# HGRN2 outer-product attention followed by a SERF feed-forward: from the ninth chunk on, the cumulative sums of log f from two 12-bit parts in float32r, logits kept for three chunks

## The chip, the cores and the metric

One core of one Trainium2 chip runs the kernel. The metric is device time in microseconds (us) of one execution, as the median of several runs.

## The reference

Inputs are q, k, v and f_logit, each of shape (4 batches, 8 heads, 768 steps, 48), and the weights w_in (384 x 2048) and w_out (2048 x 384). Per batch and head a 48x48 state is carried over the 768 steps:

```python
f = 1 / (1 + exp(-f_logit))
state = f[t][:, None] * state + outer(k[t], v[t])
y[t] = q[t] @ state
```

The 8 heads of 48 are put side by side to 3072 tokens of 384 numbers (x), and these go through

```python
h = x @ w_in
g = h * erf(softplus(h))
out = g @ w_out
```

## The kernel before, in words

**Units.** The steps of a batch are taken in chunks of 128 tokens, numbered 0 to 23 over the four batches (`g`). Two chunks are a block of 256 tokens (`CPB = 2`, `TB = 256`), so there are 12 blocks.

**A chunk's attention** goes through five steps:

- `prepare` makes log(1/f) of the logits in place: `clamp` (VectorE, L363), then `logs`, an Exp (ScalarE, L371) and a Ln (L372), on both chunks of a block at a time (128x768) except at the start. `logs` first loads another activation table (L351).
- `stage_d` (L386) takes the cumulative sums over the tokens of each half chunk as one product with a triangle of ones, `tri` (L391, 128x128 by 128x384, float32, into `ps_d`). ScalarE makes exp(-sum) (`dp`, L394) and exp(sum) (`kd`, L397) of it, eight small DMAs on the queue of SyncE (SP) carry each chunk's total decays to `Tall` (L402), and VectorE multiplies with q and k (`qd` L406, `kd` L410).
- `stage_t` transposes `qd` and `kd` on TensorE (L422) and copies the results out (L429, L433). It also runs the second half of the state update of the chunk before (`late`).
- `stage_s` makes the state's increments (L469) and the scores (L477), masks the scores (VectorE L505, by a triangle `tri1`), and updates the state (`next_state`: VectorE L446 and L447, then two GpSimd copies L449 into `sv`).
- `stage_y` makes y from scores, v and state (L534) into `xT`. The left operand `sv` holds v, which DMAs put there, beside the state.

**The feed-forward.** `hidden` makes h = x @ w_in for a block in four groups (L596). The activation of a group is a generator stepped by `act_step`: Exp (L157), two Tanh (L160), two products (VectorE L165), a Tanh (L568), a last product (VectorE L570). `project_first` (L686, blocks 0 and 1) and `project` (L737, the others, with seven products of half blocks in place of eight, from sums made by VectorE at L624) multiply by w_out; the results are put together at L745 and L753 and stored (L663).

**Order.** Each engine runs its own instructions in program order, which is written out by hand. In iteration `it` (0 to 11) a generator yields once for each product or two of the feed-forward; the slot number `s` counts these, and the steps of the attention, the loads and the steps of the activation are placed at given slots. Iteration `it` runs the attention of block `it + 2`, the hidden products of block `it + 1`, the projection of block `it - 2` and the logarithms of block `it + 3`. From iteration 4 on the slots of the attention's steps are

```python
at = [2, 26, 42, 54, 76, 90]   # d of the odd chunk, t, y and s, d of the next block's even chunk, t, y and s
```

`prepare_at` is the slot of that second `stage_d` less 14: `clamp` runs at `prepare_at - 6`, `logs` at `prepare_at`.

**Loads.** q, k, v, f_logit and w_in, w_out come by DMAs from the SP queue, in program order, except two at the start. The logits of a block lie in a tile `lt` of two chunks, of which there are two (`lpool`, four chunks in all). They are loaded (`load_f`, L229) in the middle of the iteration before the one that takes their logarithms. The weights are loaded in 16 pieces (L296) and put together from 64-bit words by ScalarE and VectorE (L315 to L340) during the first 130 us.

Of the kernel before, what the change touches and what calls it, by code (L numbers as in the profile page):

```python
# [42 lines left out]

FP32 = mybir.dt.float32
I32 = mybir.dt.int32
U32 = mybir.dt.uint32
U8 = mybir.dt.uint8
# [27 lines left out]
def kernel(  # L75
# [32 lines left out]

    def fixed(name, shape, dtype=FP32, pool=const):
        return pool.tile(shape, dtype, name=name)  # L110
# [58 lines left out]

    main = ExitStack()  # L170
    fix = main.enter_context(tc.tile_pool(name="fix", bufs=1))
    lpool = main.enter_context(tc.tile_pool(name="lpool", bufs=2))
# [46 lines left out]
    FIRST = 3  # L219


    lts = {}

    def load_f(g):
        b, c = divmod(g, NCH)
        blk, j = divmod(g, CPB)
        if j == 0:
            lts[blk] = lpool.tile([P, CPB, d_model], FP32, name="lt", tag="lt")
        nc.sync.dma_start(  # L229
            out=lts[blk][:, j, :].rearrange("t (h d) -> t h d", d=D), in_=heads(f_logit, b, c)  # L230
        )

    def load(g, what="qkv", queue=None):
        b, c = divmod(g, NCH)
# [9 lines left out]
    def half(c):  # L244
        return slice(C * c, C * (c + 1))

    def load_sv(g):
        b, n = divmod(g, NCH)
        for r in range(2):
            for c in range(2):  # L250
                to = svs[g % NSV][half(1 - r), r, c, :, PAD : PAD + D]
# [107 lines left out]
        sets[0] = 0  # L359

    def clamp(blk, j0, j1):
        lt = lts[blk][:, j0:j1, :].rearrange("t j c -> t (j c)")
        nc.vector.tensor_scalar(  # L363
            out=lt, in0=lt, scalar1=LOGIT_MIN, scalar2=None, op0=ALU.max
        )

    def logs(blk, j0, j1):

        lt = lts[blk][:, j0:j1, :].rearrange("t j c -> t (j c)")
        use_exp_ln()  # L370
        nc.scalar.activation(out=lt, in_=lt, func=AF.Exp, scale=-1.0)  # L371
        nc.scalar.activation(out=lt, in_=lt, func=AF.Ln, bias=1.0)  # L372
# [12 lines left out]
    def stage_d(g):  # L385
        blk, j = divmod(g, CPB)  # L386
        if g < FIRST:
            ps = ps_moe.tile([P, 2, 512], FP32, name="ps_d0", tag="moe")[:, 0, 0:d_model]
        else:
            ps = ps_at.tile([P, 512], FP32, name="ps_d", tag="at")[:, 0:d_model]  # L390
        nc.tensor.matmul(ps, lhsT=tri[:], rhs=lts[blk][:, j, :], start=True, stop=True)  # L391
        dp = dps[g % 2]
        kd = kds[g % 2][:, :, 0:D]
        nc.scalar.activation(  # L394
            out=dp[:, :, 0:D], in_=ps.rearrange("t (h d) -> t h d", d=D), func=AF.Exp, scale=-1.0
        )
        nc.scalar.activation(out=kd, in_=ps.rearrange("t (h d) -> t h d", d=D), func=AF.Exp)  # L397
        if g >= FIRST:
            for c in range(2):
                end = C * (c + 1)  # L400
                for a in range(HP):
                    nc.sync.dma_start(  # L402
                        out=Tall[:, g, c, a : a + 1],
                        in_=dp[end - 1 : end, 2 * a : 2 * a + 2, :].rearrange("o r d -> o (r d)"),
                    )
        nc.vector.tensor_tensor(  # L406
            out=qd[:, :, 0:D], in0=qns[g % NQ][:].rearrange("t (h d) -> t h d", d=D),
            in1=dp[:, :, 0:D], op=ALU.mult,
        )
# [27 lines left out]
    def next_state(k, dS):  # L437

        g, c = divmod(k, 2)
        g1, c1 = divmod(k + 1, 2)  # L440
        total = Tall[0:STATE, g, c, :].unsqueeze(2).broadcast_to((STATE, HP, D))
        add = dS[0:STATE, c, :].rearrange("p (a d) -> p a d", a=HP)
        if k % (2 * NCH) == 0:
            nc.vector.tensor_tensor(out=state[0:STATE], in0=add, in1=total, op=ALU.mult)
        else:
            nc.vector.tensor_tensor(out=state[0:STATE], in0=add, in1=state[0:STATE], op=ALU.add)  # L446
            nc.vector.tensor_tensor(out=state[0:STATE], in0=state[0:STATE], in1=total, op=ALU.mult)  # L447
        for r in range(2):
            nc.gpsimd.tensor_copy(  # L449
                out=svs[g1 % NSV][rows(r), r, c1, :, PAD : PAD + D], in_=state[rows(r)]  # L450
            )

    def stage_s(g):
        b, n = divmod(g, NCH)
        last = n == NCH - 1
        if n == 0:
            for r in range(2):
                nc.gpsimd.memset(svs[g % NSV][rows(r), r, 0, :, PAD : PAD + D], 0.0)
# [34 lines left out]
        for c in range(2):  # L493
            for r in range(2):
                if FIRST <= g < 2 * ADJACENT:

                    nc.scalar.copy(out=qA[half(1 - r), r, :, half(c)], in_=sc[half(c), r])
                    if c == 1:
                        flat = qA[half(1 - r), r].rearrange("s a (c t) -> s (a c) t", c=2)
                        nc.gpsimd.affine_select(  # L500
                            out=flat, in_=flat, pattern=[[0, 2 * HP], [1, C]], compare_op=ALU.is_ge,
                            fill=0.0, base=0, channel_multiplier=-1,
                        )
                    continue
                nc.vector.tensor_tensor(  # L505
                    out=qA[half(1 - r), r, :, half(c)], in0=sc[half(c), r],
                    in1=tri1[half(c)].unsqueeze(1).broadcast_to((C, HP, C)), op=ALU.mult,
                )
        next_state(2 * g, dS)
        if not last:  # L510
# [2 lines left out]
    def stage_y(g):  # L513
# [17 lines left out]
        for n in range(len(todo[0])):  # L531
            for i in todo:
                c, kt, a, r, o = todo[i][n]
                nc.tensor.matmul(  # L534
                    y[M * i : M * (i + 1), kt, half(c)], lhsT=sv[:, r, c, a, o : o + M],
                    rhs=qA[:, r, a, half(c)], start=(n == 0), stop=True, skip_group_check=True,
                )
        nc.scalar.copy(out=xTs[blk][:, :, j * P : (j + 1) * P], in_=y[:])  # L538
# [280 lines left out]
    with tc.manual_schedule():  # L819

        for t in svs:
            nc.vector.memset(t[:].rearrange("p r c a d -> p (r c a d)"), 0.0)
        use_exp_ln()
        load_f(0)
        load(0, "kv", nc.scalar)
# [6 lines left out]
        load(2)  # L832
        load_piece(1)
        load_piece(2)
        load_f(3)
# [52 lines left out]
        keep_busy(10)  # L888
        prepare(0, 0, 1)
        stage_d(0)  # L890
        keep_busy(6)
        prepare(0, 1, 2)
        stage_t(0)
# [1 line left out]
        load_piece(3)  # L895
        stage_d(1)
        prepare(1, 0, 1)
        load_f(4)
        load_f(5)
        load_sv(0)  # L900
        stage_s(0)
        weights_steps(2)
# [1 line left out]
        load(4, "qk")  # L904
        load_piece(4)
        stage_d(2)
        load_sv(1)
        weights_steps(2)
        stage_y(0)
# [30 lines left out]
        for it in range(n_blocks):  # L940
# [16 lines left out]
            for s, _ in enumerate(gen):  # L957
# [6 lines left out]
                if at and s == at[0]:  # L964
                    at.popleft()
                    f, g = todo.popleft()
                    f(g)
                    if f in (stage_y, stage_y_s):
                        if g + NSV < n_chunks:
                            load_sv(g + NSV)  # L970
                        load_to(g + LOOK)
                        if g == 2:
                            load(5, "v")
                            load_piece(7)
                if it == 0 and s == 14:
                    prepare(2, 0, CPB)
                if it == 0 and s == 9:
                    load_f(6)
                    load_f(7)
                if s == n // 2 and it + 4 < n_blocks:  # L980
                    for j in range(CPB):
                        load_f((it + 4) * CPB + j)
                if it + 3 < n_blocks and s == prepare_at - 6:
                    clamp(it + 3, 0, CPB)
                if it + 3 < n_blocks and s == prepare_at:
                    logs(it + 3, 0, CPB)
                if it < 2:
                    step = it == 1 and s % 6 == 3
                elif it == 2:
# [240 lines left out]
```

## Time and profile before

| | |
|---|---|
| median of 3 runs | 612.42 us (612.28 to 612.85) |
| the profiled execution | 612.61 us, of which its span is 610.9 us |
| TensorE (PE) busy | 588.6 us, 96% of the span |
| VectorE (DVE) busy | 428.7 us, 70% |
| ScalarE (ACT) busy | 382.7 us, 63% |
| GpSimd (POOL) busy | 92.8 us, 15% |
| mean granted clock of TensorE | 0.984 of full speed |
| HBM read and written | 35.59 and 4.72 MB |

The profile is of one execution. Times are in us from its start unless marked ns. PE are TensorE's matrix products, PEld its loads of the left operand, which run beside them; SPq is the DMA queue of SyncE. A float32 product on PE stands in the profile as two MATMUL instructions, each with its weight load. "idle before <-" names the releaser of the idle time just before an instruction. In lines of groups, xN is the number of instructions, followed by busy time and mean duration.

### The profile page before, as it was taken

What the parts mean: (1) busy time and instruction counts of PE and PEld (TensorE: products, weight loads), DVE (VectorE), ACT (ScalarE), POOL (GpSimd) and SP (SyncE); (2) the same over time, 40 slices, a digit from 0 to 9 for tenths busy, and PEclk for the clock granted to TensorE, in tenths of its full rate; (3) what the DMA queues carried; (4) which work ended last, traced back from release to release, by engine and by line L of the source; (5) the groups of instructions that cost most, each with busy time, mean ns of one, the idle gap of its engine ahead of it and who ended that gap; (6) DMA issues with size and microseconds to landing.
All of it is one profiled execution on the core that took longest, in us unless ns stands there. A gap on an engine that the chain in (4) does not pass through costs nothing.

```text
span 610.9 us, 13911 instructions
## 1 busy us (share of the span) xinstructions
PE 588.6 (96%) x5729; PEld 514.6 (84%) x5729; DVE 428.7 (70%) x702; ACT 382.7 (63%) x483; POOL 92.8 (15%) x121
## 2 busy tenths in 40 slices
PE   8797999998999999999999999999999899999996
PEld 7575888887656789989989989989989889989996
DVE  4888996674697588777777586767685675657551
ACT  5834566978875688856766767856856466266000
POOL 1333032234123101302002200102001200000000
PEclk9978999999999999999999999999999999999999
DMA  9998854431221322412412413313211000000000
GB/s 209 259 235 232 225 137 80 80 54 32 49 53 28 79 38 42 80 36 45 80 33 47 77 30 53 71 35 55 53 28 14 2 27 0 27 1 1 27 27 30
DMA packets 155605, 41.37 MB, mean 68 GB/s; under 512 B 147344, under 2 KB 150416, under 8 KB 155536
## 3 DMA queue, kind: packets, MB, share of 16 engines
q1 hardware_dynamic: 153312, 39.82, 29.8%
q8 instruction: 47, 0.77, 0.5%
q10 hardware_dynamic: 2224, 0.59, 0.4%
q14 instruction: 22, 0.18, 0.1%
HBM read 35.59 MB, written 4.72 MB: 66 GB/s over the span
## 4 chain that ended last, share of the span: by engine, by line
PE 81%; DVE 7%; ACT 7%; issue 2%; POOL 2%; ACTq 0%; POOLq 0%; DVEq 0%
PE hps L596 37%; PE ops L737 25%; PE ops L686 5%; PE y L534 3%; PE ps_t L422 3%; PE ps_d L391 2%; PE sc L477 2%; PE sc L469 2%; POOL sv L449 2%; ACT x L160 1%; DVE qA L505 1%; DVE Hg L570 1%; ACT e L568 1%; PE busy L383 1%; ACT e L157 1%
## 5 line engine op out<-in xcount | busy, mean ns | idle before, releaser
L596 PE MATMUL hps<-xT,w_in_sb 128*128 128x256 f32 x1152 | 266.1, 387 | 2.4 <-ACT xT L538 1.2
L596 PEld LDWEIGHTS hps<-xT,w_in_sb 128*128 128x128 f32 x1152 | 219.2, 193 | 36.6 <-ACT xT L538 1.9
L165 DVE SCALAR_TENSOR_TENSOR e<-x,e 128x1024 f32<-128x1024 f32 x96 | 117.2, 1221 | 13.9 <-ACT x L160 13.8
L449 POOL COPY sv<-state 48x192 f32<-48x192 f32 x88 | 76.3, 867 | 319.0 <-DVE state L447 222.9
L160 ACT ACTIVATE x<-Hg,serf_bias 128x1024 f32<-128x1024 f32 x88 | 97.5, 1141 | 0.2
L157 ACT ACTIVATE e<-Hg 128x1024 f32<-128x1024 f32 x44 | 46.5, 1058 | 52.3 <-DVE Hg L570 48.3
L737 PE MATMUL ops<-wT,Hg 128*128 128x192 f32 x320 | 78.4, 328 | 0.0
L570 DVE TENSOR_TENSOR Hg<-Hg,e 128x1024 f32<-128x1024 f32 x44 | 53.7, 1221 | 24.6 <-ACT e L568 24.5
L737 PE MATMUL ops<-wT,scratch 128*128 128x192 f32 x288 | 67.8, 326 | 0.9 <-DVE scratch L745 0.9
L603 ACT COPY Hg<-hps 128x1024 f32<-128x1024 f32 x44 | 44.4, 1010 | 36.2 <-PE hps L596 35.8
L737 PE MATMUL ops<-w_out_sb,Hg 128*128 128x192 f32 x320 | 65.1, 326 | 0.0
L737 PEld LDWEIGHTS ops<-wT,Hg 128*128 128x128 f32 x320 | 55.7, 190 | 1.9
L737 PEld LDWEIGHTS ops<-w_out_sb,Hg 128*128 128x128 f32 x320 | 54.6, 190 | 2.0
L505 DVE TENSOR_TENSOR qA<-sc,tri 64x256 f32<-64x256 f32 x68 | 28.7, 422 | 34.1 <-PE sc L477 33.1
L568 ACT ACTIVATE e<-e 128x1024 f32<-128x1024 f32 x48 | 50.3, 1048 | 1.9 <-DVE e L165 1.8
L737 PEld LDWEIGHTS ops<-wT,scratch 128*128 128x128 f32 x288 | 50.2, 190 | 1.1 <-issue 1.1
L745 DVE TENSOR_TENSOR scratch<-scratch,ops 128x384 f32<-128x384 f32 (+1 forms) x40 | 19.9, 497 | 33.4 <-ACT scratch L753 26.0
L406 DVE TENSOR_TENSOR qd<-qn,dp 128x384 f32<-128x384 f32 x24 | 13.9, 580 | 39.0 <-ACT dp L394 39.0
L534 PEld LDWEIGHTS y<-qA,sv 128*32 128x32 f32 x1536 | 24.3, 111 | 19.6 <-issue 8.9
L534 PE MATMUL y<-qA,sv 128*32 128x64 f32 x1536 | 29.0, 222 | 10.8 <-POOL sv L449 5.1
L429 ACT COPY qA<-ps_t 64x512 f32<-64x512 f32 x48 | 27.7, 577 | 16.9 <-PE ps_t L422 16.6
L737 PE MATMUL ops<-w_out_sb,scratch 128*128 128x192 f32 x132 | 32.2, 326 | 0.0
(118 smaller groups left out, 653.2 us busy)
## 6 DMA issues: line engine op xcount, KB each, us to landing
lt<-in_f_logit_dram SPq DMA_DIRECT2D x24, 192.0 KB, 3.8
qn<-in_q_dram SPq DMA_DIRECT2D x24, 192.0 KB, 3.2
kn<-in_k_dram SPq DMA_DIRECT2D x23, 192.0 KB, 3.5
vt<-in_v_dram SPq DMA_DIRECT2D x23, 192.0 KB, 3.7
out_dram<-scratch SPq DMA_DIRECT2D x11, 384.0 KB, 2.6
sv<-in_v_dram SPq DMA_DIRECT2D x84, 48.0 KB, 2.9
w_out_sb<-in_moe_w_in_dram SPq DMA_DIRECT2D x4, 768.0 KB, 6.0
Hg<-in_moe_w_in_dram SPq DMA_DIRECT2D x4, 768.0 KB, 6.3
```

The lines of the kernel that those rows point to most:

```text
L157: nc.scalar.activation(out=dst[:], in_=h, func=AF.Exp)
L160: nc.scalar.activation(out=dst[:], in_=h, func=AF.Tanh, bias=serf_bias[:, i : i + 1], scale=SERF_KAB[i][0])
L165: nc.vector.scalar_tensor_tensor(out=e[:], in0=x[:], scalar=SERF_KAB[i][2], in1=e[:], op0=ALU.add, op1=ALU.mult)
L449: nc.gpsimd.tensor_copy(out=svs[g1 % NSV][rows(r), r, c1, :, PAD : PAD + D], in_=state[rows(r)])
L505: nc.vector.tensor_tensor(out=qA[half(1 - r), r, :, half(c)], in0=sc[half(c), r], in1=tri1[half(c)].unsqueeze(1).broadcast_to((C, HP, C)), ...
L534: nc.tensor.matmul(y[M * i : M * (i + 1), kt, half(c)], lhsT=sv[:, r, c, a, o : o + M], rhs=qA[:, r, a, half(c)], start=(n == 0), stop=Tru ...
L568: nc.scalar.activation(out=e[:], in_=e[:], func=AF.Tanh, scale=SERF_C)
L570: nc.vector.tensor_tensor(out=h, in0=h, in1=e[:], op=ALU.mult)
L596: nc.tensor.matmul(hps[:, j, :], lhsT=w_in_sb[:, kt, ft * P : (ft + 1) * P], rhs=xTs[blk][:, kt, :], start=(kt == 0), stop=(kt == n_k - 1),)
L603: nc.scalar.copy(out=gr["h"], in_=hps[:])
L686: nc.tensor.matmul(ops[:, tt, 0:d_model], lhsT=gr["h"][:, j, tt * P : (tt + 1) * P], rhs=w_out_sb[:, ft, :], start=(ft == 0), stop=(ft == ...
L737: nc.tensor.matmul(place[n], lhsT=x[:, j, :], rhs=y, start=(gi == 0 and j == 0 and n in first), stop=(gi == n_g - 1 and j == 1), skip_grou ...
```

## The change

From block 4 (`SPLIT`), that is from chunk 8 of 0 to 23, log(1/f) is split before the triangular product: a VectorE copy rounds it to float32r (the upper part), a VectorE subtraction leaves the remainder (the lower part, also float32r), and `stage_d` sums the two products of `tri_r`, the triangle in float32r, in one PSUM tile. Blocks 0 to 3 keep the one float32 product. The first part's copy and subtraction stand in program order right behind `logs` of the block; those of the second chunk stand 18 slots later, because there is one buffer `parts` for both.

The logits lie in a ring of three chunks, in place of two tiles of two. Their loads move: chunk 3 behind `stage_d(0)`, chunks 4 and 5 behind `stage_d(2)`, chunk 7 from slot 9 of iteration 0 to slot 36, chunks 8 and 9 from slot 48 to slot 78, and both chunks of blocks 5 to 11 from the middle of the iteration before to just behind the first `stage_d` of the iteration that uses them, behind that step's eight small DMAs.

The tiles `sv` are packed closer (272 in place of 320 numbers for a part), and the mask of the scores is read from `tri` in place of a copy `tri1`.

```diff
-    tri1 = fixed("tri1", [P, C])
+    tri_r = fixed("tri_r", [P, P], FP32R)
...
-    svs = [fixed(f"sv{i}", [P, 2, 2, HP, D + 2 * PAD], pool=fix) for i in range(NSV)]
+    svs = [fixed(f"sv{i}", [P, 2, 2, HP * DP + PAD], pool=fix) for i in range(NSV)]
...
+    SPLIT = 4
+    NL = 3
+    lring = fixed("lt", [P, NL, d_model], pool=fix)
+    parts = fixed("parts", [P, 2, d_model], FP32R, pool=fix)
+
+    def lt_of(blk, j0, j1):
+        if blk == SPLIT:
+            return lring[:, 2 * j0 : 2 * j1 - 1 : 2, :]
+        s = (CPB * blk + j0) % NL if blk < SPLIT else j0
+        assert s + j1 - j0 <= NL
+        return lring[:, s : s + j1 - j0, :]
...
+    def split(g):
+
+        blk, j = divmod(g, CPB)
+        x = lt_of(blk, j, j + 1)[:, 0]
+        nc.vector.tensor_copy(out=parts[:, 0], in_=x)
+        nc.vector.tensor_tensor(out=parts[:, 1], in0=x, in1=parts[:, 0].bitcast(FP32), op=ALU.subtract)
...
-        nc.tensor.matmul(ps, lhsT=tri[:], rhs=lts[blk][:, j, :], start=True, stop=True)
+        if blk < SPLIT:
+            nc.tensor.matmul(ps, lhsT=tri[:], rhs=lt_of(blk, j, j + 1)[:, 0], start=True, stop=True)
+        else:
+            for i in range(2):
+                nc.tensor.matmul(ps, lhsT=tri_r[:], rhs=parts[:, i], start=(i == 0), stop=(i == 1))
...
-                    in1=tri1[half(c)].unsqueeze(1).broadcast_to((C, HP, C)), op=ALU.mult,
+                    in1=tri[half(c), half(c)].unsqueeze(1).broadcast_to((C, HP, C)), op=ALU.mult,
...
-        for c in range(2):
-            nc.gpsimd.tensor_copy(out=tri1[half(c), :], in_=tri[half(c), half(c)])
+        nc.gpsimd.tensor_copy(out=tri_r[:], in_=tri[:])
...
                     f, g = todo.popleft()
                     f(g)
+                    if f is stage_d and g % CPB and SPLIT < it + 3 < n_blocks:
+                        for j in range(CPB):
+                            load_f((it + 3) * CPB + j)
...
                 if it == 0 and s == 9:
                     load_f(6)
+                if it == 0 and s == 36:
                     load_f(7)
-                if s == n // 2 and it + 4 < n_blocks:
-                    for j in range(CPB):
-                        load_f((it + 4) * CPB + j)
+                if it == 0 and s == 78:
+                    load_f(8)
+                    load_f(9)
                 if it + 3 < n_blocks and s == prepare_at - 6:
                     clamp(it + 3, 0, CPB)
                 if it + 3 < n_blocks and s == prepare_at:
                     logs(it + 3, 0, CPB)
+                    if it + 3 >= SPLIT:
+                        split((it + 3) * CPB)
+                if SPLIT <= it + 3 < n_blocks and s == prepare_at + 18:
+                    split((it + 3) * CPB + 1)
```

More of the change, by code (lines that the diff above doesn't have):

```diff
@@ L44 @@
 FP32 = mybir.dt.float32
+FP32R = mybir.dt.float32r
 I32 = mybir.dt.int32
@@ L171 @@
     fix = main.enter_context(tc.tile_pool(name="fix", bufs=1))
-    lpool = main.enter_context(tc.tile_pool(name="lpool", bufs=2))
     work = main.enter_context(tc.tile_pool(name="work", bufs=2))
@@ L187, with sv_rows @@
     NSV, PAD = 2, DP - D
-    svs = [fixed(f"sv{i}", [P, 2, 2, HP, D + 2 * PAD], pool=fix) for i in range(NSV)]
+    svs = [fixed(f"sv{i}", [P, 2, 2, HP * DP + PAD], pool=fix) for i in range(NSV)]
+    def sv_rows(g, part, r, c):
+        return svs[g % NSV][part, r, c, 0 : HP * DP].rearrange("p (a d) -> p a d", d=DP)[:, :, PAD:]
     qns = [fixed(f"qn{i}", [P, d_model], pool=fix) for i in range(NQ)]
@@ L219 @@
     FIRST = 3
-    lts = {}
+    SPLIT = 4
[8 more added lines that the diff above has]
+        return lring[:, s : s + j1 - j0, :]
     def load_f(g):
@@ L226, in load_f @@
         blk, j = divmod(g, CPB)
-        if j == 0:
-            lts[blk] = lpool.tile([P, CPB, d_model], FP32, name="lt", tag="lt")
         nc.sync.dma_start(
-            out=lts[blk][:, j, :].rearrange("t (h d) -> t h d", d=D), in_=heads(f_logit, b, c)
+            out=lt_of(blk, j, j + 1).rearrange("t j (h d) -> t (j h) d", d=D), in_=heads(f_logit, b, c)
         )
+    def split(g):
[3 more added lines that the diff above has]
+        nc.vector.tensor_tensor(out=parts[:, 1], in0=x, in1=parts[:, 0].bitcast(FP32), op=ALU.subtract)
     def load(g, what="qkv", queue=None):
@@ L250, in load_sv @@
             for c in range(2):
-                to = svs[g % NSV][half(1 - r), r, c, :, PAD : PAD + D]
+                to = sv_rows(g, half(1 - r), r, c)
                 if g < FIRST:
@@ L361, in clamp @@
     def clamp(blk, j0, j1):
-        lt = lts[blk][:, j0:j1, :].rearrange("t j c -> t (j c)")
+        lt = lt_of(blk, j0, j1)
         nc.vector.tensor_scalar(
@@ L367, in logs @@
     def logs(blk, j0, j1):
-        lt = lts[blk][:, j0:j1, :].rearrange("t j c -> t (j c)")
+        lt = lt_of(blk, j0, j1)
         use_exp_ln()
@@ L449, in next_state @@
             nc.gpsimd.tensor_copy(
-                out=svs[g1 % NSV][rows(r), r, c1, :, PAD : PAD + D], in_=state[rows(r)]
+                out=sv_rows(g1, rows(r), r, c1), in_=state[rows(r)]
             )
@@ L457, in stage_s @@
             for r in range(2):
-                nc.gpsimd.memset(svs[g % NSV][rows(r), r, 0, :, PAD : PAD + D], 0.0)
+                nc.gpsimd.memset(sv_rows(g, rows(r), r, 0), 0.0)
         qA, kT = qAs[g], kTs.pop(g)
@@ L534, in stage_y @@
                 nc.tensor.matmul(
-                    y[M * i : M * (i + 1), kt, half(c)], lhsT=sv[:, r, c, a, o : o + M],
+                    y[M * i : M * (i + 1), kt, half(c)], lhsT=sv[:, r, c, DP * a + o : DP * a + o + M],
                     rhs=qA[:, r, a, half(c)], start=(n == 0), stop=True, skip_group_check=True,
@@ L821 @@
         for t in svs:
-            nc.vector.memset(t[:].rearrange("p r c a d -> p (r c a d)"), 0.0)
+            nc.vector.memset(t[:].rearrange("p r c d -> p (r c d)"), 0.0)
         use_exp_ln()
@@ L834 @@
         load_piece(2)
-        load_f(3)
         nc.gpsimd.memset(tri[:], 1.0)
@@ L890 @@
         stage_d(0)
+        load_f(3)
         keep_busy(6)
@@ L897 @@
         prepare(1, 0, 1)
-        load_f(4)
-        load_f(5)
         load_sv(0)
@@ L906 @@
         stage_d(2)
+        load_f(4)
+        load_f(5)
         load_sv(1)
```

## The prediction

> **What bounds the kernel now.** I read the page's totals first, then the chain that ended last.
>
> ```profile
> PE 588.6 (96%) x5729; PEld 514.6 (84%) x5729; DVE 428.7 (70%) x702; ACT 382.7 (63%) x483; POOL 92.8 (15%) x121
> PE 81%; DVE 7%; ACT 7%; issue 2%; POOL 2%; ACTq 0%; POOLq 0%; DVEq 0%
> ```
>
> TensorE is busy 96% of the span, and the chain is 81% PE. A mean hides stages, so the chain in order of time comes next, cut at the twelfth chunk's `stage_d` (columns: start, us, what).
>
> ```profile
> 184.28 0.84 PE ops L686 x2
> 185.12 0.65 PE ps_d L391 x2
> 185.77 9.03 PE ops L686 x28
> 194.80 0.87 PE ps_t L422 x8
> ```
>
> Each piece starts where the last one ended. The list of PE's waits from 185 to 480 us is empty, so what PE sheds there the end moves by. One triangular product occupies PE for 0.65 us, the distance of its start from the next piece's. Of the 16 chunks changed, 11 to 23 (13 of them) have theirs between 185.1 and 465.7 us; 8, 9 and 10 have theirs at 115.8, 131.0 and 151.3. Before 185 PE does wait, as the timeline says (start, us, engine and line, what, then idle before and releaser):
>
> ```profile
> 141.96 1.21 DVE L570 TENSOR_TENSOR wT<-wT,e 128x1024 f32<-128x1024 f32 x1
> 143.20 1.06 ACT L157 ACTIVATE e<-wT 128x1024 f32<-128x1024 f32 x1 [2.08 <-DVE wT L570]
> ...
> 145.54 1.21 PE L534 MATMUL y<-qA,sv 128*32 128x64 f32 x64 [0.91 <-POOL sv L449]
> ...
> 169.53 1.21 PE L534 MATMUL y<-qA,sv 128*32 128x64 f32 x64 [0.93 <-POOL sv L449]
> ```
>
> There the chain runs through DVE and ACT, and PE arriving earlier waits longer.
>
> **The product.** Removed: 0.65 us of PE per chunk. Added: two float32r products. The trace has no float32r product. The remote row above is the float32 product itself: if each part costs as much, the pair takes 1.30, 0.65 more than now. The nearest instruction is half a float32 product, 0.325: the pair then takes 0.65, no gain. Below, the chain's eight transposes take 0.87, 0.109 each with a weight load for each, and nothing in the trace loads 128x128 weights faster: the pair takes 0.22, a gain of 0.43. I take a quarter of the float32 product. A 24-bit operand is two halves of 12 bits, so a full product is four partial ones in 0.65 us, 0.1625 each (an estimate); a part of 12 bits against ones and zeros needs one of them. Two parts: 0.325, a gain of 0.325 per chunk. Times 13: 4.2 us. The three early products get nothing, since their 1.0 us falls ahead of the wait at 169.53; the ends are 0 and 1.0.
>
> The Trainium skill, FP8 and Floating Point Precision, section TensorE Precision Notes, gives true FP32 as four passes through the array and a reduced FP32 that is read as 4 bytes and truncated; by it a part is one pass, and the sum would be the same 4.2 us. No row of this trace shows the reduced form.
>
> **The split.** DVE gets a copy and a subtraction for each of 16 chunks. Rows by shape:
>
> ```profile
> L363 DVE TENSOR_SCALAR lt<-lt 128x384 f32<-128x384 f32 x4 | 1.4, 352 | 0.0
> L624 DVE TENSOR_TENSOR wT<-w_out_sb,wT 128x384 f32<-128x384 f32 x8 | 4.4, 555 | 0.3
> ```
>
> Copy as the first, subtraction as the second: 0.9 us, 14.5 in all, on an engine that idles some 14 us in each 50 of the steady stage. The harm would come from order. The first split stands behind the Ln of ACT, and DVE's queue stops until that has ended:
>
> ```profile
> 435.58 0.84 ACT L372 ACTIVATE lt<-lt 128x768 f32<-128x768 f32 x1
> ...
> 436.10 1.73 DVE L505 TENSOR_TENSOR qA<-sc,tri 64x256 f32<-64x256 f32 x4 [1.53 <-PE sc L477]
> ...
> 441.64 0.56 DVE L406 TENSOR_TENSOR qd<-qn,dp 128x384 f32<-128x384 f32 x1 [3.03 <-ACT dp L394]
> ```
>
> Ln ends at 436.42, the split at 437.3, so the mask L505 and the state behind it come 1.2 us later. The `y` that needs them runs at 457.1, and the 3.03 us wait at 441.64 takes the delay up. Without that cover a 1.2 us delay in each of six iterations would be 7 us on DVE, still not on PE until `y`'s lead is gone. The second split waits for the first `stage_d` to have read `parts`; that product is at 439.97, and DVE gets there after 442.6 (busy with L745), so nothing waits, and 0.9 us falls ahead of the state update at 450.16, whose `y` is at 457.1. In iterations 1 and 2 the splits fall beside waits of 3.33 (115.42), 1.24 (125.89), 6.25 (154.12) and 2.32 us (158.80) of DVE. I charge nothing; the ends are 0 and 1.0.
>
> A rule against the change stands in the Trainium skill, SBUF — State Buffer, Who interferes with whom: a VectorE copy in its two-port form, or an operation with two SBUF inputs, and a GpSimd copy lock each other out for a whole instruction. Pairs of L449 take 0.74 us alone and 4.19 at 415.45, beside L165 and L570, which agrees. If by the rule the splits held up both copies behind PE's waits at 145.54 and 169.53, it would be 1.8 us more.
>
> **The later loads.** From block 5 on the logits are issued behind the eight `Tall` DMAs of the first `stage_d`, about 5 us on SP's queue, and `clamp` then waits on DVE. A load lands 2.9 us after issue at least, 3.8 in the median; the second issues 0.6 after the first. Iteration 3:
>
> ```profile
> 186.32 5.04 SPq L402 DMA_DIRECT2D Tall<-dp  x8
> 189.97 0.55 DVE L363 TENSOR_SCALAR lt<-lt 128x768 f32<-128x768 f32 x1
> 190.44 1.22 DVE L165 SCALAR_TENSOR_TENSOR e<-x,e 128x1024 f32<-128x1024 f32 x1
> 192.30 0.36 DVE L446 TENSOR_TENSOR state<-sc,state 112x192 f32<-112x192 f32 x1 [0.64 <-POOL sv L449]
> 192.69 0.36 DVE L447 TENSOR_TENSOR state<-state,Tall 112x192 f32<-112x192 f32 x1
> 195.71 0.69 DVE L433 COPY kT<-ps_t 128x512 f32<-128x512 f32 x1 [2.66 <-PE ps_t L422]
> 196.32 1.22 DVE L570 TENSOR_TENSOR Hg<-Hg,e 128x1024 f32<-128x1024 f32 x1
> ```
>
> Both have landed at 191.36 + 0.6 + 2.9 to 3.8 = 194.9 to 195.8, so `clamp` stands still for 5 to 6 us where it now runs at 189.97. Behind it queue L165, the state, the copy `kT` and the last product of a group. They would end near 197.4, 198.1, 198.8 and 200.0. PE wants `kT` for the scores at 203.0, that group from 203.5, the state at 224.8: a lead of 3.5 us. I charge nothing; with the slowest landing of the page, 7.5 us, the group ends at 203.8 and PE waits under 1 us. In iteration 2 `Tall` ends at 137.36, the logits land at 140.9 to 141.8, and `clamp` now runs at 141.49: up to 0.3 us, ahead of the L570 at 141.96 for which ACT waits; charged in full. In iterations 4 to 8 `clamp` comes 10.9 to 13.6 us after the product, the landing 10.1 to 11.0: nothing. SP has nothing urgent behind these loads: its next are those at `y`. Chunks 8 and 9 issue at 98.1, land by 102.6, and are wanted at 104.1.
>
> **Start-up and layout.** Chunk 3's load keeps its place in the queue, since the product it now waits for is done at 7.7 and SP reaches it at 14.4. Chunks 4 and 5 go behind a weight piece; they are wanted at 47.8, and the piece goes up to 1.9 us earlier. Two memsets of 1125 ns shrink by 15%, 0.3 us together. The mask's other stride and the `sv` stride cost nothing that a row tells. Value 0; ends a gain of 0.5 and a loss of 0.2.
>
> **The sum.** 4.2 - 0.3 = 3.9 us. Against the profiled execution's own 612.61 (span 610.9 and 1.7 around it) that is 608.7; the median is 0.2 lower: 608.5.
>
> **The rivals.** About 0.2%, 1.2 us, is what a measurement of this kernel can tell from no change: faster means below 611.2, slower above 613.6.
>
> First, slower: the float32r product runs no faster than a float32 one, and there are two. The place is the `ps_d` pair of each chunk on PE, the price 0.65 for 13 chunks, 8.5 us: 621. It decides as soon as one part takes over 0.325 us. For it: no row shows a faster product of this shape. Against: the trace splits a float32 product into two instructions, so an operand of half the width should need less.
>
> Second, no change: a part takes as long as one of those two instructions, 0.325. Nothing is gained, 0.3 is lost at `clamp` and a little on DVE: 612.4 to 613.4.
>
> Third, the gain is made and given back: iteration 3's blocked DVE outlasts its lead of 3.5 us, or ACT's eviction of `hps` slips behind DVE. Two to three us come back: 611. Against it: PE has no wait at all after 185, and DVE has waits of 1.5 to 5 us throughout.
>
> **How the numbers follow.** The gain 0.72, the slow product 0.10, the half-width one 0.12, given back 0.06. The first alone spans 606.4 (parts of 0.11 us, 5.6, and 0.4 at the start) to 610.5 (all the ends of cost). To leave out no more than 2 in 10 the range goes to 612.8, over the third rival and half of the second. Faster: 0.71 and half of the third, 0.74. Slower: the first rival and a quarter of the second, 0.13. The same: 0.13.
>
> **What would show it.** Right: the chain has `ps_d` pieces of about 0.33 us from chunk 11 on; the iterations, which now begin 46.4 us apart (280.70 and 327.08), are 45.7 apart; PE has no new wait after 185; `clamp` in iteration 3 waits some 5 us for DMA. Wrong: pieces of 0.65 or more, a PE wait on `kT` or `Hg` near 203, or a wait for the logits in the steady iterations.

## The result, and the profile after

The changed kernel takes 614.95 us (median of 9 runs, 614.18 to 618.93) beside 612.68 us for the kernel before on the same chip: a ratio of 1.0041 [1.0023, 1.0060], 2.3 us slower. The forecast was 608.5 us. The profiled execution took 616.11 us, 1.2 above its median, with a span of 614.3.

In the changed kernel the line numbers move: the product is L414, the split L249 and L250, `clamp` L382, Exp and Ln L390 and L391, the mask L528, Exp of a group L158, products of a group L166 and L593, `dp` L417, `qd` and `kd` L429 and L433, hidden products L619, `project`'s sums L768.

The page's totals, and the chain's shares by engine:

```profile
PE 586.1 (95%) x5729; PEld 515.1 (84%) x5729; DVE 441.2 (72%) x734; ACT 383.0 (62%) x483; POOL 103.6 (17%) x120
PE 62%; DVE 5%; ACT 3%; issue 2%; POOL 1%; DMA 0%; SPq 0%; ACTq 0%; POOLq 0%
```

TensorE (PE) works 2.5 us less and VectorE (DVE) 12.5 us more, and the span is 3.4 us longer: PE has lost more in waiting than it saved. The shares of the two chains can't be set side by side: the changed kernel's is followed back only to 164.7 us, while the other's shares come to 99% of the span. The product itself did what was forecast. The chain in order of time at the twelfth chunk:

```profile
185.47 0.84 PE ops L709 x2
186.31 0.35 PE ps_d L414 x2
```

The pair takes 0.35 us where one float32 product took 0.65. Where nothing waits, two such gains shorten an iteration from 46.39 to 45.79 us. But the list of PE's waits between 185 and 485 us, empty before, now reads (total us, times, longest):

```profile
PE hps L619 <- DVE scratch L768: 2.1, 2, 1.7
PE sc L500 <- issue: 1.2, 1, 1.2
PE y L557 <- issue: 0.5, 1, 0.5
```

The new groups (busy us, mean ns, idle before them):

```profile
L249 DVE CAST parts<-lt 128x384 fp32r<-128x384 f32 x16 | 5.7, 355 | 19.8 <-ACT lt L391 19.8
L250 DVE TENSOR_TENSOR parts<-lt,parts 128x384 fp32r<-128x384 f32 x16 | 9.0, 561 | 0.7
```

A split costs 0.92 us, and DVE stood still before the copies for 19.8 us in all, waiting for Ln. How that reaches PE shows in the chain of waits in iteration 4 (start, us, what):

```profile
252.23 0.85 ACT lt L391
...
253.11 0.37 DVE parts L249
...
253.50 0.56 DVE parts L250
...
254.09 0.07 DVE qA L528
...
256.60 1.14 DVE e L166
257.74 1.15 DVE Hg L593
...
259.87 0.48 ACT dp L417
...
260.95 0.55 DVE kd L433
261.50 0.47 DVE scratch L768
...
262.58 0.36 DVE scratch L768
...
263.08 1.97 PE hps L619 x8
```

Read it from below. The second group of hidden products cannot start until the third sum of L768 has emptied a PSUM buffer. The sums stand behind `qd` and `kd`, these wait for `dp`, which stands on ACT behind the Exp L158 and the Tanh of a group, and that Exp waits for the product L593. L593 stands on DVE behind the mask, and the mask behind the split, which waits for Ln. Each of these engines runs its instructions in order, so a delay of the split reaches all of them. Counted from d13 (the start of chunk 13's triangular product), the mask starts at 16.8 us before and 18.0 after, and the first of the sums at 24.1 and 25.3: the 1.2 us arrive. PE had some lead here, and waits 0.45 us. In iteration 6 the price is larger. The timeline (start, us, engine and line, what, idle before and releaser), after, and then the same place of before:

```profile
345.37 0.36 DVE L249 CAST parts<-lt 128x384 fp32r<-128x384 f32 x1 [2.48 <-ACT lt L391]
350.04 1.06 ACT L158 ACTIVATE e<-Hg 128x1024 f32<-128x1024 f32 x1 [4.33 <-DVE Hg L593]
353.95 0.56 DVE L429 TENSOR_TENSOR qd<-qn,dp 128x384 f32<-128x384 f32 x1 [2.81 <-ACT dp L417]
354.90 1.52 DVE L768 TENSOR_TENSOR scratch<-scratch,ops 128x384 f32<-128x384 f32 x3
356.57 4.12 PE L619 MATMUL hps<-xT,w_in_sb 128*128 128x256 f32 x18 [1.69 <-DVE scratch L768]
```

```profile
346.73 1.06 ACT L157 ACTIVATE e<-Hg 128x1024 f32<-128x1024 f32 x1 [2.99 <-DVE Hg L570]
350.64 0.56 DVE L406 TENSOR_TENSOR qd<-qn,dp 128x384 f32<-128x384 f32 x1 [2.82 <-ACT dp L394]
351.59 1.53 DVE L745 TENSOR_TENSOR scratch<-scratch,ops 128x384 f32<-128x384 f32 x3
```

ACT waits 1.34 us longer for the group's product, and 4.9 us after its Exp the sums start in both kernels. The wait of `qd` for `dp` between them is 2.82 us before and 2.81 after: it takes nothing up, and the delay goes through whole.

The stages of PE, from one triangular product to another (d11 is chunk 11's), in us, worked out from the starts of PE's instructions in each profile. The last column is the start of PE's last instruction; the 112.71 us ahead of it, which begin near 497 (487 to 500), are alike in all. Up to d8 the profiles differ by as much as 2.7 us, nearly all of it in their first 75 us and also between kernels that are alike up to there; that column is no measure of the change.

| kernel | to d8 | d8–d11 | d11–d13 | d13–d15 | d15–d17 | d17–d19 | d19–d23 | d23–497 | last start |
|---|---|---|---|---|---|---|---|---|---|
| before | 115.81 | 69.15 | 48.54 | 46.39 | 46.39 | 46.67 | 92.78 | 26.97 | 605.40 |
| after | 115.05 | 70.81 | 50.28 | 46.49 | 45.79 | 47.70 | 91.73 | 28.44 | 609.01 |
| e1 ring only | 114.72 | 69.47 | 48.53 | 46.39 | 46.39 | 46.66 | 92.78 | 28.65 | 606.29 |
| e2 split unused | 115.53 | 70.82 | 48.92 | 46.76 | 46.39 | 47.98 | 92.78 | 26.97 | 608.85 |
| e3 product | 116.59 | 70.03 | 50.17 | 45.80 | 45.80 | 46.36 | 91.60 | 26.81 | 605.87 |
| e4 split later | 115.15 | 70.09 | 48.77 | 46.45 | 45.79 | 47.57 | 91.57 | 26.80 | 604.91 |
| e6 loads earlier | 114.66 | 70.78 | 50.56 | 46.48 | 45.80 | 47.71 | 91.72 | 26.81 | 607.23 |
| e8 logs earlier | 114.94 | 68.97 | 50.48 | 49.76 | 45.88 | 49.61 | 92.12 | 28.48 | 612.93 |
| e10 GpSimd split | 115.05 | 69.47 | 48.73 | 45.80 | 45.81 | 46.36 | 92.09 | 26.81 | 602.84 |
| e11 e10 and loads | 116.11 | 69.47 | 48.72 | 45.79 | 45.82 | 46.36 | 92.09 | 26.80 | 603.87 |
| e12 slot 58 | 115.14 | 70.82 | 50.53 | 45.79 | 45.80 | 45.78 | 91.59 | 25.19 | 603.33 |
| e13 both | 115.06 | 69.46 | 48.73 | 45.80 | 45.79 | 45.78 | 91.58 | 25.19 | 600.10 |
| e14 before, slot 58 | 115.69 | 69.19 | 48.54 | 46.39 | 46.39 | 46.38 | 92.78 | 25.35 | 603.42 |
| e15 unused, slot 58 | 117.37 | 70.85 | 48.84 | 46.39 | 46.39 | 46.38 | 92.78 | 25.35 | 607.05 |

After against before: the gain holds only in d15–d17 and d19–d23. It loses 1.7 us in d8–d11, 1.7 in d11–d13 and 1.0 in d17–d19. The 1.5 of d23–497 is a stretch at half clock in the profiled execution (491.5 to 494.9 us); e1, without any split, has one there too, so it is no part of the change's price.

### The profile page after: what moved, and what is told of

Its sections match the earlier page's. It is cut to its first block, busy times and chain, and to the rows that moved or that the text cites. A ratio compares the mean times of both kernels' runs of the same rounds, so it can differ in the third digit from the quotient of the medians.

```text
span 614.3 us, 13925 instructions
## 1 busy us (share of the span) xinstructions
PE 586.1 (95%) x5729; PEld 515.1 (84%) x5729; DVE 441.2 (72%) x734; ACT 383.0 (62%) x483; POOL 103.6 (17%) x120
## 4 chain that ended last, share of the span: by engine, by line
PE 62%; DVE 5%; ACT 3%; issue 2%; POOL 1%; DMA 0%; SPq 0%; ACTq 0%; POOLq 0%
PE hps L619 26%; PE ops L760 24%; PE ops L709 5%; PE y L557 2%; PE ps_t L445 2%; PE sc L500 1%; DVE Hg L593 1%; PE sc L492 1%; POOL sv L472 1%; DVE scratch L768 1%; ACT x L161 1%; DVE qA L528 1%; PE ps_d L414 1%; DVE scratch L647 1%; DVE e L166 1%
## 5 line engine op out<-in xcount | busy, mean ns | idle before, releaser
L619 PE MATMUL hps<-xT,w_in_sb 128*128 128x256 f32 x1152 | 267.6, 388 | 4.6 <-DVE scratch L768 2.1
L619 PEld LDWEIGHTS hps<-xT,w_in_sb 128*128 128x128 f32 x1152 | 219.9, 194 | 38.6 <-issue 2.3
L472 POOL COPY sv<-state 48x192 f32<-48x192 f32 x88 | 87.4, 993 | 308.7 <-DVE state L470 216.9
L166 DVE SCALAR_TENSOR_TENSOR e<-x,e 128x1024 f32<-128x1024 f32 x96 | 117.1, 1220 | 13.5 <-ACT x L161 13.4
L158 ACT ACTIVATE e<-Hg 128x1024 f32<-128x1024 f32 x44 | 46.5, 1058 | 60.6 <-DVE Hg L593 55.6
L593 DVE TENSOR_TENSOR Hg<-Hg,e 128x1024 f32<-128x1024 f32 x44 | 53.7, 1220 | 20.3 <-ACT e L591 20.3
L768 DVE TENSOR_TENSOR scratch<-scratch,ops 128x384 f32<-128x384 f32 (+1 forms) x40 | 19.9, 497 | 34.6 <-ACT scratch L776 26.6
L528 DVE TENSOR_TENSOR qA<-sc,tri 64x256 f32<-64x256 f32 x68 | 28.7, 422 | 15.8 <-PE sc L500 14.7
L429 DVE TENSOR_TENSOR qd<-qn,dp 128x384 f32<-128x384 f32 x24 | 13.9, 579 | 35.2 <-ACT dp L417 35.2
```

The source lines that it names most:

```text
L158: nc.scalar.activation(out=dst[:], in_=h, func=AF.Exp)
L166: nc.vector.scalar_tensor_tensor(out=e[:], in0=x[:], scalar=SERF_KAB[i][2], in1=e[:], op0=ALU.add, op1=ALU.mult)
L472: nc.gpsimd.tensor_copy(out=sv_rows(g1, rows(r), r, c1), in_=state[rows(r)])
L528: nc.vector.tensor_tensor(out=qA[half(1 - r), r, :, half(c)], in0=sc[half(c), r], in1=tri[half(c), half(c)].unsqueeze(1).broadcast_to((C, ...
L593: nc.vector.tensor_tensor(out=h, in0=h, in1=e[:], op=ALU.mult)
L619: nc.tensor.matmul(hps[:, j, :], lhsT=w_in_sb[:, kt, ft * P : (ft + 1) * P], rhs=xTs[blk][:, kt, :], start=(kt == 0), stop=(kt == n_k - 1),)
```

## The experiments

The theory: the splits on DVE delay the order behind them. A first rival: the later loads and the ring do, through the blocked `clamp`. A second: the float32r product, or the layout, costs something on PE.

**e1 and e2: the ring alone, and the splits without their use.** In both, the float32 product reads the ring; e1 also has no split.

```diff
-        if blk < SPLIT:
-            nc.tensor.matmul(ps, lhsT=tri[:], rhs=lt_of(blk, j, j + 1)[:, 0], ...)
-        else:
-            ... two products of parts
+        nc.tensor.matmul(ps, lhsT=tri[:], rhs=lt_of(blk, j, j + 1)[:, 0], start=True, stop=True)
```

> The changed kernel without the split and with the float32 product: ring of three chunks, later loads and closer sv remain. Theory A (the gain on PE is real, and VectorE's order around the split gives back more than it): the loads alone cost under 1 us and the start gains 0.5, so 612 to 613.3 us beside 612.7 before. Theory B (the later loads lose the time, through clamp standing for the DMA): 615 us or more. Theory C (the float32r products cost elsewhere what they save): about 612.5 us.

> As the changed kernel, with both splits made and never read: each triangular product is the float32 one of the logarithms. Theory A: the splits' cost stands alone on top of the first experiment, 617 to 620 us (615 and the 16 x 0.30 that PE no longer gains). Theory B or C: like the first experiment within 1 us.

e1: 613.31 us beside 613.18, 0.9995 [0.9980, 1.0010]. Ring, loads and layout together cost nothing that these runs can tell; the first rival falls. e2: 616.49 beside 613.18, 1.0055 [1.0035, 1.0074]. Splits that nobody reads cost 3.2 us over e1 (3.7 by the two ratios, each known to 0.2%). The stages of e2 and e1 say where: 1.36 and 0.39 in d8–d11 and d11–d13, 0.37 and 1.32 in d13–d15 and d17–d19, 3.4 together. So half of the price falls before iteration 4 and half in iterations 4 and 6. The list of PE's waits from 185 to 485 us in e2, where that sum is L764, has the wait of iteration 6 as the changed kernel has it:

```profile
PE hps L615 <- DVE scratch L764: 1.4, 1, 1.4
```

**e3: the product alone.** Only chunk 8 is split, and all later chunks use its parts.

```diff
-                    if it + 3 >= SPLIT:
+                    if it + 3 == SPLIT:
                         split((it + 3) * CPB)
-                if SPLIT <= it + 3 < n_blocks and s == prepare_at + 18:
-                    split((it + 3) * CPB + 1)
```

> The changed kernel with one split alone, of chunk 8; all later chunks sum that chunk's parts again, so their decays are those of chunk 8. VectorE has none of the other 15 splits. Theory A: 607 to 608.7 us, the whole gain of 16 x 0.30 with the start's 0.5. Theory B: 612 or more. Theory C: 612 or more, with new waits on PE around the products.

612.05 beside 613.18, 0.9982 [0.9961, 1.0002]: no gain that is clear of the noise, where 607 to 608.7 was expected. The stages say more: from d13 on the 0.6 per iteration is there, but for 0.3 us in d17–d19, so the second rival has nothing there. Up to d13 it is lost: 0.9 us in d8–d11, of which e1 without any split has 0.3, and the one split that is left is the likely rest; and 1.6 in d11–d13, mostly by a stall told of at the end.

**e4: the first split four slots later.** It no longer stands ahead of the mask.

```diff
-                    if it + 3 >= SPLIT:
-                        split((it + 3) * CPB)
+                if SPLIT <= it + 3 < n_blocks and s == prepare_at + 4:
+                    split((it + 3) * CPB)
```

> The changed kernel with the first split of each block four slots later, so that from iteration 4 on it stands behind the mask and the state update and no longer holds these up until Ln has ended. Theory A, if the wait on Ln is the larger part: 610 to 612.5 us, and PE's waits on L768 at 263 and 356 us are gone. Theory A, if the 14.5 us of work on VectorE is the larger part, or theory B: 613.5 to 615.5 us, with these waits still there.

614.40 beside 613.18, 1.0031 [1.0008, 1.0053]. The mask is free, but another wait takes the place. Timeline of iteration 6, DVE and PE:

```profile
346.41 1.22 DVE L166 SCALAR_TENSOR_TENSOR e<-x,e 128x1024 f32<-128x1024 f32 x1
347.55 0.35 DVE L249 CAST parts<-lt 128x384 fp32r<-128x384 f32 x1
348.05 0.97 PE L414 MATMUL ps_d<-parts,tri_r 128*128 128x384 f32 x2 [1.18 <-DVE parts L249]
```

The split now stands behind two long products, and PE waits for the split itself. In this profile it is the only PE wait from 185 to 485 us beside one of 0.5. The profiled execution is the fastest of twelve (611.97 us), so its stages stand for the kernel's best and not for its median. With 0.9 us of work to place on DVE, early delays the mask and late delays the product.

**e6: the loads of two chunks earlier,** issued behind the second split of the iteration before in place of behind the first `stage_d`.

```diff
-                    if f is stage_d and g % CPB and SPLIT < it + 3 < n_blocks:
-                        for j in range(CPB):
-                            load_f((it + 3) * CPB + j)
...
+                    if it + 4 < n_blocks:
+                        for j in range(CPB):
+                            load_f((it + 4) * CPB + j)
```

> The changed kernel with the logits of blocks 5 to 11 loaded right behind the second split of the iteration before, so that clamp never waits for them. Theory D (PE is the bound only by a small lead; each delay of VectorE or ScalarE uses the lead up, and at chunk 11 the 4.8 us that clamp stands makes y wait and then PE's next instructions come late): PE's waits at 225.9 and 228.2 us go, about 2 us less than the changed kernel, ratio to before 0.998 to 1.002. Theory E (the loads are harmless, as the first experiment's equal time says, and only the split costs): ratio 1.003 to 1.005, like the changed kernel.

615.43 beside 613.09, 1.0042 [1.0018, 1.0066]: as the change itself, and PE's waits of 0.5 and 1.4 us in d11–d13, which the blocked `clamp` was suspected of, are still there. The loads are out of it a second time.

**e8: the logarithms 8 slots earlier,** with e6's loads, so that DVE need not wait for Ln.

```diff
+                ahead = 8 if it > 1 else 0
-                if it + 3 < n_blocks and s == prepare_at:
+                if it + 3 < n_blocks and s == prepare_at - ahead:
                     logs(it + 3, 0, CPB)
-                    if it + 3 >= SPLIT:
-                        split((it + 3) * CPB)
+                if SPLIT <= it + 3 < n_blocks and s == prepare_at:
+                    split((it + 3) * CPB)
```

(`clamp` moves as `logs` does.)

> As the experiment before, and from iteration 2 on clamp and logs stand 8 slots earlier while the split keeps its slot, so that Ln has ended when VectorE comes to the split. If the wait on Ln is what the split costs in the steady iterations: PE's waits on L768 at 263 and 356 us go as well, another 2 us less, ratio to before 0.994 to 0.998. If it is the 0.9 us of work for each split: no less than the experiment before.

617.61 beside 613.09, 1.0067 [1.0042, 1.0091]: worse. The wait for Ln is gone, and DVE waits for something else at the same place, as the timeline of iteration 4 says:

```profile
249.90 2.19 ACT L161 ACTIVATE x<-Hg,serf_bias 128x1024 f32<-128x1024 f32 x2
252.47 0.55 DVE L768 TENSOR_TENSOR scratch<-scratch,ops 128x384 f32<-128x384 f32 x1 [5.62 <-ACT scratch L776]
253.33 0.56 DVE L250 TENSOR_TENSOR parts<-lt,parts 128x384 fp32r<-128x384 f32 x1
253.91 1.73 DVE L528 TENSOR_TENSOR qA<-sc,tri 64x256 f32<-64x256 f32 x4
262.90 5.81 PE L619 MATMUL hps<-xT,w_in_sb 128*128 128x256 f32 x18 [2.03 <-DVE scratch L768]
```

ACT, done early with Ln, runs two Tanh ahead of the eviction L776. Counted from d13 of the same kernel (234.4 here, 236.1 in the changed kernel, by the table's sums), the mask starts at 19.5 us, later than the changed kernel's 18.0, and PE waits 2.03 us. So the wait for Ln is not the cause by itself; the lateness of mask and last product is, whatever causes it.

**e10 and e11: both operations of the split on GpSimd;** e11 has e6's loads too.

```diff
-        nc.vector.tensor_copy(out=parts[:, 0], in_=x)
-        nc.vector.tensor_tensor(out=parts[:, 1], in0=x, ...)
+        nc.gpsimd.tensor_copy(out=parts[:, 0], in_=x)
+        nc.gpsimd.tensor_tensor(out=parts[:, 1], in0=x, ...)
```

> The changed kernel with both operations of the split on GpSimd instead of VectorE, at the same places; loads as in the changed kernel. If the cost is VectorE's time and order: like the kernel with one split alone, ratio 0.996 to 1.0. If GpSimd is too slow for it (rows of this trace: 0.29 us for a cast of 128 columns, so about 0.9 us for 384, and the sv copies queue behind): d or y waits for GpSimd, ratio 1.003 or more.

> The split on GpSimd and the loads right behind the second split of the iteration before. Theory D: both costs are gone and most of the gain of 16 x 0.30 stays, ratio 0.992 to 0.996. If GpSimd holds up the sv copies: above 1.0, with PE waiting on GpSimd's sv.

e10: 609.97 beside 613.09, 0.9952 [0.9932, 0.9973], faster. e11: 611.30, 0.9962 [0.9945, 0.9979]; its loads add nothing. GpSimd takes 1.5 us or more for a split (0.50 and 1.00 in most, up to 1.4 and 1.9), longer than DVE, and it hardly matters: PE waits for a part once, 0.3 us. Timeline of iteration 4 in e10:

```profile
249.86 1.73 DVE L528 TENSOR_TENSOR qA<-sc,tri 64x256 f32<-64x256 f32 x4 [1.82 <-PE sc L500]
250.59 0.50 POOL L249 CAST parts<-lt 128x384 fp32r<-128x384 f32 x1 [3.60 <-issue]
251.18 1.00 POOL L250 TENSOR_TENSOR parts<-lt,parts 128x384 fp32r<-128x384 f32 x1
253.45 1.21 DVE L593 TENSOR_TENSOR Hg<-Hg,e 128x1024 f32<-128x1024 f32 x1
254.40 9.23 PE L619 MATMUL hps<-xT,w_in_sb 128*128 128x256 f32 x42
```

The mask starts before the split, 16.6 us after d13 (18.0 in the changed kernel), L593 comes 20.2 us after it (21.6), and the 42 hidden products run in one piece. The same product and the same loads with the splits off DVE: the theory stands. Waits for the sums are left, two of 0.3 us, as PE comes earlier now.

**e12 to e15: the other end of the chain.** If the last sums hold PE because they stand behind `qd` and `kd`, moving the second `stage_d` by four slots puts them ahead. `clamp`, `logs` and splits keep their slots.

```diff
-                at = ... else [2, 26, 42, 54, 76, 90]
+                at = ... else [2, 26, 42, 58, 76, 90]
-                prepare_at = at[todo.index((stage_d, (it + 3) * CPB))] - 14
+                prepare_at = at[todo.index((stage_d, (it + 3) * CPB))] - (14 if it < 4 else 18)
```

e12 does this to the changed kernel, e13 to e10, e14 to the kernel before (the control), e15 to e2.

> The changed kernel with stage_d of each block's even chunk at slot 58 instead of 54 from iteration 4 on, so that the three last sums of the projection (L768), which free the PSUM that the second group of hps takes, stand ahead of qd and kd on VectorE and no longer behind ScalarE's dp; clamp, logs and both splits keep their slots. If the steady iterations lose their time through that chain (split, mask, last product of a group, ScalarE's queue, dp, qd, kd, L768, hps): PE's waits at 263 and 356 us go, with what the clock adds to them, ratio to before 0.997 to 1.001 where the changed kernel has 1.004. If they lose it in another way: 1.003 to 1.005.

> As the experiment before, and both operations of the split on GpSimd. Both covers together: ratio 0.992 to 0.995. If GpSimd's split alone has already removed that chain: the same as with it alone, 0.995 within 0.001.

> The kernel before the change with the later slot 58 (the fourth step of each iteration from 4 on; in iteration 9 the fourth step is the last y, which then also runs 4 slots later). The control for the two experiments before. Their profile shows the stretch around the last y 1.8 us shorter (25.2 us from the last d to the fixed point after it, 27.0 before), and before has one wait of 0.3 us on L745 at 353. If the later slot alone gives that: ratio 0.996 to 0.9975, and the steady iterations stay at 46.4 us. If it did nothing for the kernel before: 0.999 to 1.001.

> Both splits made and never read, float32 products, and the later slot. If the chain over L768 is what the splits cost in the steady iterations: these are at 46.4 us like the control's, and what is left of the splits' cost is that of the chunks before iteration 4, 1 to 1.5 us: ratio 0.998 to 1.0, where the same without the later slot had 1.0055. If the splits cost by their work: 1.002 or more.

| kernel | us | before, same chip | ratio |
|---|---|---|---|
| e12 | 609.70 | 612.23 | 0.9950 [0.9932, 0.9969] |
| e13 | 607.64 | 612.23 | 0.9923 [0.9906, 0.9940] |
| e14 | 610.79 | 612.65 | 0.9962 [0.9950, 0.9975] |
| e15 | 612.50 | 612.65 | 0.9992 [0.9981, 1.0003] |

In e12 the sums come before `qd`, with the split still on DVE and still ahead of the mask. Timeline of DVE:

```profile
253.84 0.56 DVE L250 TENSOR_TENSOR parts<-lt,parts 128x384 fp32r<-128x384 f32 x1
260.26 1.52 DVE L768 TENSOR_TENSOR scratch<-scratch,ops 128x384 f32<-128x384 f32 x3
262.04 0.55 DVE L429 TENSOR_TENSOR qd<-qn,dp 128x384 f32<-128x384 f32 x1
```

PE has no wait for L768 left, and every iteration from d13 on is 45.79. That shows the chain from its other end. But the control e14 gains 0.38% by the slot alone, since the last `y` also moves, for which PE waits 1.6 us in every kernel with slot 54 and not at all with slot 58 (d23–497 from 26.97 to 25.35), and the kernel before sheds its own 0.3 us of d17–d19. Against e14, e12 is 0.12% faster (0.9950 / 0.9962), which is within the intervals, and e13 0.39%, 2.4 us. e15 against e14 is 0.30% slower, 1.8 us: with the steady stage cured, this is what the splits cost before iteration 4 (d8–d11 1.66 and d11–d13 0.30 longer than e14's; of the 1.66 the ring alone has 0.3 in e1). e13 is the fastest version, below both kernels.

## Why the prediction was wrong

**The product: right.** Forecast 0.325 us for the pair and a gain of 0.325; measured 0.35 and 0.30. Rivals one and two (slow product, half-rate product) fall with it. That the three early products gain nothing held: d8–d11 gave none of their 0.9 us. That all thirteen others gain did not: d11–d13 lost more than its share, and the 0.6 each of d13–d15 and d17–d19 went into waits.

**Loads and start: right in the main.** `clamp` in iteration 3 waits for its DMA nearly as forecast (4.83 us beside 5 to 6), and PE does not notice, as e1 and e6 show:

```profile
196.07 0.56 DVE L382 TENSOR_SCALAR lt<-lt 128x768 f32<-128x768 f32 x1 [4.83 <-DMA lt<-in_f_logit_dram]
```

The 0.3 us charged at `clamp` of iteration 2 did not come that way: it starts there at 142.04 with no wait. But d8–d11 is 0.3 us longer in e1 and e10 than before, and no run shows by what part of the new layout or loads. The first hidden product starts at 27.87 us in place of 28.39, but other profiles with the changed start have 27.42 to 28.20, so whether the start gained can't be told.

**The split: the step that failed.** Its size was right (0.9 forecast, 0.92 measured), and so was the delay of the mask (1.2 forecast, 1.2 measured); "I charge nothing; the ends are 0 and 1.0" was wrong by 3.2 us (e2 over e1). Two reasons were given. The first: "the 3.03 us wait at 441.64 takes the delay up". That line is of iteration 8, and there it held. After the change the same `qd` waits

```profile
444.20 0.56 DVE L429 TENSOR_TENSOR qd<-qn,dp 128x384 f32<-128x384 f32 x1 [1.69 <-ACT dp L417]
```

and starts 22.2 us after d21, where it started at 22.3 before. But this one iteration was taken for all six. In iteration 8 the Exp ahead of `dp` starts 17.2 us after d21, ahead of the mask, so its group doesn't stand behind the split. In iterations 4 and 6 the group's product stands behind the mask, the Exp and `dp` behind that product, and the wait of `qd` for `dp` comes 1.2 us later and keeps its length (0.37 us in iteration 4; 2.82 before and 2.81 after in iteration 6). A wait takes up a delay only if what it waits for isn't delayed too. The second: "still not on PE until `y`'s lead is gone". The mask's reader was taken to be `y`, 20 us on, but on an engine that runs in order everything queued behind the mask is delayed as well, above all L593, then ACT's Exp, then `dp`, then the sums that free PSUM. And an empty list of PE's waits gave no lead: in iteration 6 it was nothing, since before's d17–d19 is already 0.28 us longer than its neighbours. Before iteration 4, "the splits fall beside waits" of DVE failed in part likewise. In e2 beside e1, DVE's wait for `dp` in iteration 2 (2.32 us) keeps its length and ends 0.8 us later after d8, and PE's waits for `sv` between 85 and 185 us are 3.5 us in place of 2.2 (1.8 before, 3.9 after the change). That the splits got there through the chain of those chunks is argued from these lengths; it wasn't followed link by link.

**The account.** Forecast -3.9 us, measured +2.3: 6.2 apart. The splits' 3.2 is one part. The other is that of the product's gain (13 times 0.30, 3.9) only some 0.9 shows, from e2's 1.0055 to the change's 1.0041, each known to 0.2%. Between the profiles of e2 and after, 2.0 us of what is missing is in d11–d13 (0.6 shorter was due, 1.36 longer came), 1.2 of it the stall told of below, whose cause stays open.

**The third rival** was the right one in kind, the gain given back through ACT and DVE, but it got a chance of 0.06, its cause was put down to the blocked `clamp` or the eviction of `hps`, and its price left over 1 us of the gain standing. No rival on the slower side was about order on DVE.

**The rule of the lock** in the Trainium skill (SBUF — State Buffer, Who interferes with whom) was priced at 1.8 us behind the waits of the two `y`. It isn't the cause there. The GpSimd copies as a group grow by 11 us in all (before L449, then after L472),

```profile
L449 POOL COPY sv<-state 48x192 f32<-48x192 f32 x88 | 76.3, 867 | 319.0 <-DVE state L447 222.9 <-DVE state L444 58.0 <-PE ps_t L422 32.4
```

```profile
L472 POOL COPY sv<-state 48x192 f32<-48x192 f32 x88 | 87.4, 993 | 308.7 <-DVE state L470 216.9 <-DVE state L467 58.2 <-PE ps_d L414 10.7
```

yet the pairs ahead of those two `y` last as long as before (4.34 and 0.75 then, 4.34 and 0.74 now; 1.60 and 3.39 both times). They only start later, by 0.5 and 1.2 us. Nor is the growth shown to be the lock of the splits: in e10, with no split on VectorE, the copies take 85.9 us.

## What to carry to other kernels

A wait on an engine is room for added work only if its releaser lies outside the chain that the work delays: follow the releaser back before calling a wait a cover. One iteration's wait doesn't speak for the others: here the same delay vanished in one and reached PE in two. A saturated engine without waits in the list may have a lead of zero, and work added to its neighbours is charged by what stands behind it in their queues, here down to where a PSUM buffer comes free. If an engine off that chain has the room, slower work there can be cheaper: here 1.5 us and more on GpSimd beat 0.92 on VectorE.

## What the runs showed of the hardware

**A wait of about 2 us can cost nearly as much again in clock.** After 7 of the 27 waits of PE over 1.5 us that the fourteen profiles show from 85 us on, the granted clock is half for about 3.4 us; these seven waits are of 1.6 to 2.3 us. The length alone does not decide: 1.61 was enough in e1, and 1.90 was not in e6. The profile of e8 has four such stretches. Stretches of e8 (columns: stretch, length, busy time and instructions of PE, PE's loads, DVE, ACT, GpSimd, clock, DMA share, GB/s). PE's wait of 2.03 us ends at 262.90, between the first and the second:

```profile
258.00:262.00 4.00, 2.87 (x14) 2.19 (x12) 3.60 (x6) 3.27 (x5) 2.38 (x2) 1.00 0.02 0
263.50:266.80 3.30, 3.30 (x10) 2.59 (x9) 3.27 (x6) 0.96 (x2) 0.00 (x0) 0.50 0.22 45
267.00:270.00 3.00, 3.00 (x19) 2.70 (x19) 2.93 (x6) 1.86 (x3) 0.00 (x0) 1.00 0.90 197
```

The 18 hidden products from 262.90 on take 5.81 us here, and 4.12 in the changed kernel's iteration 6 (both lines stand above): the stretch costs about 1.7 us. That fits the wide scatter of the kernels with such waits (e8 613.9 to 622.1 us; e13, with no wait over 1.4, 607.1 to 609.2). The Trainium skill (TensorE: Matmul & The Clock Gate, Part 1: The HAM clock gate) describes a half-rate state and a free-running window of 3.4 us; rate and length agree, but it asks for an idle window of about 3.4 us, and here waits of half to two thirds of that were enough.

**A stall without a releaser.** In d11–d13, PE stalls for 1.2 to 1.4 us in the middle of the scores (after, e3, e6, e8 and e12):

```profile
229.32 0.33 PE L500 MATMUL sc<-qA,kT 48*64 48x64 f32 x3 [1.17 <-issue]
```

In these the 16 KB fetch of instructions that falls there (queue q8) starts when PE is at its product 2296 (2281 in e8); in the other nine kernels, none of which stalls, it starts at 2209 to 2211. So fetch and stall go together in all fourteen profiles. That the fetch causes it is only argued, and what makes it late is open: `y` ahead of it is as late in e4 and e10, which do not stall. No run set out to move it.
